# A fused retention and snake-activation kernel on one core: a new hand-written order for the first three blocks, a different order inside the loop, and a re-cut last tile

## The chip, the cores and the metric

The kernel runs on one core of one Trainium2 chip. The metric is the device time in microseconds of one execution. The program is one long instruction stream per engine: TensorE (PE, with PEld for its weight loads), VectorE (DVE), ScalarE (ACT), GpSimd (POOL) and SyncE (SP), which here issues most DMAs. Each engine runs its own stream strictly in order and waits on semaphores for the others.

## The reference

```python
def _attn_ref(q, k, v):                      # 8 batches, 8 heads, 576 tokens, 64 wide
    scores = (1 / sqrt(64)) * q @ k^T
    gamma = 1.0 - 2.0 ** (-5.0 - arange(H))  # one decay per head
    Dmat = where(rel >= 0, gamma ** rel, 0)  # rel = position of query - position of key
    return (scores * Dmat) @ v

def _moe_ref(x, w_in, w_out, alpha):         # x: 4608 tokens x 512
    h = x @ w_in                             # 512 x 2048
    s = sin(alpha * h)
    g = h + s * s / (alpha + 1e-09)
    return g @ w_out                         # 2048 x 512
```

Inputs and output are float32. The attention output of all heads, put side by side, is x.

## The kernel before, in words

**Tiling.** The 4608 tokens are nine blocks of 512. Block n (0 to 7) is the first 512 tokens of batch n; block 8 is the last 64 tokens of all eight batches (the class `Ends`). The attention is written as linear attention over chunks of 128 tokens: inside a chunk it is scores, a causal mask and values; between chunks it is a running state. The class `Attention` holds the pieces of one batch, each a burst of small TensorE matmuls of 64x64 weights: `scores(p, y)` for half p of the batch and half y of the heads (16 matmuls, L318), `outer` for the sums k^T v of the chunks (L266), `values(p, False)` and `values(p, True)` for the masked scores times v (16 matmuls each, L356), and `add_states(p)` for the contribution of the running state (L374). VectorE masks the scores (`masked`, L329). `evict`, `take_sum`, `next_sum`, `more`, `to_state` and `chain` turn the sums of the chunks into states, on ScalarE, VectorE or GpSimd. `keep` casts the result into `xT`, the input of the block's projection.

The two `values` of one half write the same PSUM bank from the two halves of the rows of the PE array; `values(p, False)` must be finished before `values(p, True)` begins. The kernel before has TensorE itself wait there: `change_rows` issues `nc.tensor.drain()`.

**The dense part.** A block has 16 units. `project(n, u)` is 4 matmuls of 512 columns (L486), `sine` is ScalarE (L494), `square` is on an engine of choice (L503 or L505), `product` is VectorE (L510) and writes `gT`. `gemm2(n, u)` is 4 matmuls (L530); four of them make one tile of 128 rows of output, which `finish` copies out of PSUM (L102 or L104) and sends by two DMAs of 64 partitions each (L523).

**Loads.** `load` brings 512 KB of q, k or v in float32 by a DMA on SP into one of six `raw` buffers (L113); `cast` scales it to float16 and frees the buffer (L161, L104). For batches 0 and 1, q and k are transposed by TensorE (`turn`, then `take` copies out); from batch 2 on by a transposing DMA on SP (`crossed`, L184). The weights come in eight pieces by DMAs on the GpSimd queue (`load_w_in` L92, `load_w_out` L95). `wait_for_w_out(g)` is a small DMA on SP that reads piece g of `w_out`, so SP goes no further before that piece has landed (L558). `keep_busy` issues matmuls on a tile of zeros whose results nobody reads (L543).

**PSUM.** Eight banks: the tag `hp` with three buffers of one bank, the tag `mm` with two buffers of two banks, the tag `op` with one bank. The buffer of a tag is the next free one.

**Order.** All of it is in a manual schedule: every engine takes its instructions in the order of the program text. Blocks 0 to 2, with the attention of batches 0 to 3 and the loads up to batch 4, are one list written out by hand (L561 to L1024). Blocks 3 to 8 are a loop (L1026 on): block n projects, the second GEMM of block n-1 follows one block behind, and the attention of batch n+1, the loads and casts of batch n+2 and the ends are hung at given units with `at_unit` (before the unit's activation work) and `behind` (after it). In the loop before, a batch's attention sits at units 0, 4, 8 and 12; its chunk sums are at unit 4:

```python
at_unit(4, lambda: A.outer((0, 1)), lambda: A.scores(1, 0), lambda: A.evict((0, 1)))
behind(4, lambda: A.chain((0, 1, 2, 3)), lambda: A.masked(1, 0))
at_unit(8, lambda: A.scores(1, 1), lambda: A.values(0, False))
at_unit(12, lambda: A.values(1, False), lambda: A.values(0, True), lambda: A.add_states(0))
```

After the loop come the 16 second-GEMM units of block 8; the last unit is cut into two column halves in one PSUM bank.

Of the kernel before, what the change touches and what calls it, by code (L numbers as in the profile page):

```python
# [1 line left out]

# [14 lines left out]
def kernel(  # L17
# [170 lines left out]
    def turn(b, nm, p, ys=(0, 1), tag="hp"):  # L188
        if (b, nm, p) not in trs:
            trs[b, nm, p] = psum.tile([P, 1024], F16, tag=tag, bufs={"hp": 3, "op": 1}[tag], name="tr")  # L190
# [18 lines left out]
    turns = nc.alloc_semaphore("turns")  # L209
    turn_of = {}  # L210
    unmarked = []

# [9 lines left out]

    class Attention:
        def __init__(self, b):
            self.b = b
            self.both = {}
            self.o = {}
            self.ret = {}
            self.sc = {}
            self.kv = {}  # L230
            self.tiles = {}

# [17 lines left out]
        def outer(self, ps, spare=False):  # L250
            b = self.b
            if spare:
                kv = [
                    psum.tile([P, 512], F32, tag=tag, bufs=3 if tag == "hp" else 1, name="kv")
                    for tag in ("op", "hp")
                ]
            else:
                kv2 = psum.tile([P, 2, 512], F32, tag="mm", bufs=2, name="kv")
                kv = [kv2[:, g] for g in range(2)]
                self.kv2 = kv2  # L260
# [14 lines left out]
        def evict(self, ps, eng=None):  # L275
# [4 lines left out]
                self.kv2[:, :, 0 : 256 * N].rearrange("p g (x y) -> p g x y", x=N),  # L280
            )
# [27 lines left out]
        def scores(self, p, y):  # L309
            kT, qT = T[self.b, "k", p], T[self.b, "q", p]  # L310
            sc = psum.tile([P, 2, 512], F32, tag="mm", bufs=2, name="sc")
# [25 lines left out]
        def values(self, p, same, spare=False):  # L337
# [3 lines left out]
            else:  # L341
                open_turns.append((self, p))
            if p not in self.o and spare:
                self.o[p] = [psum.tile([P, 512], F32, tag="hp", bufs=3, name="o") for t in range(2)]
            elif p not in self.o:
                self.both[p] = psum.tile([P, 2, 512], F32, tag="mm", bufs=2, name="o")
                self.o[p] = [self.both[p][:, t] for t in range(2)]
            o, v16 = self.o[p], half[self.b, "v", p]
            for x in range(2):
                for r in range(2):  # L350
                    for e in range(2):
                        for g in range(2):
# [3 lines left out]
                            matmul(  # L356
# [4 lines left out]
                            )  # L361
# [32 lines left out]
    class Ends:  # L394


        def __init__(self, j0):
            self.js = (j0, j0 + 1)
            self.o = {}

        def scores(self):
            self.sc = psum.tile([P, 2, 512], F32, tag="mm", bufs=2, name="scs")
# [22 lines left out]
        def values(self, w, same):  # L425
            if same:
                change_rows((self, w))
            else:
                open_turns.append((self, w))
            if w not in self.o:  # L430
                self.o[w] = psum.tile([P, 2, 512], F32, tag="mm", bufs=2, name="os")
            o, v16 = self.o[w], half[2 * self.js[w], "v", 2]
            for x in range(2):
                for e in range(2):
                    for g in range(2):
                        t = g if same else 1 - g
                        c = 128 * x + 64 * g
                        matmul(
                            o[halves(e), t, c : c + 64],
                            v16[halves(g), 4 * t + 2 * x + e, :],  # L440
                            self.ret[halves(g), t, w, 2 * x + e, :],
                            start=(not same and x == 0), stop=False, skip_group_check=True,
                        )

        def add_states(self, w):
            o, j = self.o[w], self.js[w]
            for g in range(2):
                for x in range(2):
                    for e in range(2):
                        for t in range(2):  # L450
                            c = 128 * x + 64 * g
                            matmul(
                                o[halves(e), t, c : c + 64],
                                sS[halves(t), 2 * j + g, 2 * x + e, :],
                                T[2 * j, "q", 2][halves(t), 2 * x + e, halves(g)],
                                start=False, stop=True, skip_group_check=True,
                            )

        def keep(self, w, eng):
# [4 lines left out]
                self.o[w][:, :, 0:256].rearrange("p t (x n) -> p t x n", x=2),  # L464
# [8 lines left out]
    def bank(tag):  # L473
        if tag == "mm":
            return psum.tile([P, 2, 512], F32, tag="mm", bufs=2, name="hps")[:, 0]
        return psum.tile([P, 512], F32, tag=tag, bufs=3 if tag == "hp" else 1, name="hps")

    def project(n, fc, part=None, tag="hp"):
# [33 lines left out]
    def rows_of(n, c, h):  # L512
        if n == 8:
            b = 2 * c + h
            return out[576 * b + 512 : 576 * b + 576, :]
        r0 = 576 * n + 128 * c
        return out[r0 : r0 + 128, :].rearrange("(i r) d -> r i d", r=2)[h]

    def finish(n, c, eng=None, cols=slice(0, 512)):
        osb = work.tile([P, 512], F32, tag="osb", bufs=4, name="osb")  # L520
        copy(eng or nc.scalar, osb[:, cols], ops[n, c][:, cols])
        for h in range(2):
            nc.sync.dma_start(rows_of(n, c, h)[:, cols], osb[halves(h), cols])  # L523

    def gemm2(n, u, tag="op", cols=slice(0, 512)):
        c, part = divmod(u, 4)
        if (n, c) not in ops:
            ops[n, c] = psum.tile([P, 512], F32, tag=tag, bufs=1 if tag == "op" else 3, name="ops")
        for fk in range(4 * part, 4 * part + 4):
            matmul(  # L530
                ops[n, c][:, cols], gT[n][:, fk, c * P : (c + 1) * P], w_out16[:, fk, cols],
                start=(fk == 0 and cols.start == 0), stop=(fk == FC - 1), skip_group_check=True,
# [7 lines left out]
    def keep_busy(n, m=512, tag="op"):  # L540
        idle = psum.tile([P, 512], F32, tag=tag, bufs=3 if tag == "hp" else 1, name="idle")
# [18 lines left out]
    with tc.manual_schedule():  # L560
# [9 lines left out]

        load(0, "k", 0)
        load(0, "q", 0)
        load(0, "k", 1)
        load(0, "q", 1)
        load(0, "v", 0)
        load(0, "v", 1)
        keep_busy(13)
        cast(0, "k", 0, V)
        turn(0, "k", 0)
        take(0, "k", 0, A_)  # L580
        keep_busy(2)
        cast(0, "q", 0, V)
        turn(0, "q", 0)
        take(0, "q", 0, V)
        keep_busy(2, tag="hp")
        at[0].scores(0, 1)
        turn_alpha()
        cast(0, "k", 1, V, (0,))
        cast(0, "k", 1, G_, (1,))
        load_w_in(0)  # L590
        take_alpha()
        at[0].scores(0, 0)
        turn(0, "k", 1)
        take(0, "k", 1, A_)
        at[0].masked(0, 0)
        cast(0, "q", 1, G_)
        load_w_in(2)
        load_w_in(1)
        keep_busy(6)
        cast(0, "v", 0, A_)  # L600
        at[0].masked(0, 1)
        turn(0, "q", 1)
        take(0, "q", 1, A_, (1,))
        take(0, "q", 1, V, (0,))
        at[0].outer((0,), spare=True)
        keep_busy(3, tag="hp")
        at[0].take_sum(0, A_)
        cast(0, "v", 1, A_)
        at[0].take_sum(1, V)
        at[0].more(1)  # L610
        at[0].to_state(1, G_)
        at[0].to_state(0, G_)
        load_w_out(0)
        load_w_in(3)
        at[0].scores(1, 0)
        at[0].scores(1, 1)
        at[0].masked(1, 0)
        at[0].masked(1, 1)
        load_w_out(1)
        keep_busy(5, tag="hp")  # L620
        at[0].outer((1,), spare=True)
        at[0].values(0, False)
# [3 lines left out]
        at[0].next_sum(2)  # L626
        at[0].to_state(2, V)
        at[0].values(1, False, spare=True)
        at[0].values(1, True, spare=True)
        at[0].add_states(1)  # L630
        invert_alpha()
        at[0].keep(1, V, A_)
        wait_for_w_out(0)
        load(1, "k", 0)
        load(1, "q", 0)
# [3 lines left out]
        load(2, "k", 0)  # L639
        project(0, 1, 0, tag="mm")  # L640
        project(0, 0, 0, tag="mm")
        project(0, 0, 1, tag="mm")
        sine(0, 0)
        at[0].next_sum(3)
        project(0, 1, 1, tag="mm")
        sine(0, 1)
        load_w_out(2)
        at[0].to_state(3, G_)
        project(0, 2, tag="op")
        sine(0, 2)  # L650
        square(0, 2, A_)
        square(0, 1, V)
        square(0, 0, V)
        project(0, 3)
# [466 lines left out]
```

## Time and profile before

| what | us |
|---|---|
| median of 3 runs (range) | 319.76 (319.76 to 322.72) |
| the profiled execution's own time | 320.69 |
| its span, first to last instruction | 318.9 |
| TensorE busy | 301.3 (94%) |
| VectorE, ScalarE, GpSimd busy | 216.9, 174.0, 137.3 |
| first projection matmul of block 0 | starts at 19.89 |
| projections of block 1 in full swing | from 59.17 |
| first projection of the loop (block 3) | 115.52 |
| blocks 3, 4, 5, 6 of the loop | 31.62, 31.58, 31.58, 31.56 each |
| last second-GEMM stretch begins | 299.44 |
| end | 318.9 |

The span is 1.79 us shorter than the execution's own time; the rest lies before the first and after the last instruction. Times inside the span are read against 318.9. TensorE's matmuls are pipelined: a matmul of 512 columns is shown with 0.38 us, and in an unbroken stream four of them start every 0.864 us, which is 0.216 us each.

### The profile page before, as it was taken

The numbers are of one execution on the slowest core, as the hardware profiler recorded it, in microseconds if no ns is written. First come the engines' busy times: TensorE is split into PE (matmuls) and PEld (weight loads), VectorE is DVE, ScalarE is ACT, GpSimd is POOL, SyncE is SP. The second block draws the span as 40 slices with busy tenths as digits, with TensorE's granted clock in tenths as the row PEclk, the third lists the DMA queues.
The fourth block names the chain that finished last, engine by engine and source line by source line (L and its number), as shares of the span: only waits on it lengthen the run. The fifth ranks groups of instructions, "written<-read, shape, count | busy, mean of one in ns | idle before, by whom it ended". The sixth has DMA issues, their size and how long they took to land.

```text
span 318.9 us, 7711 instructions
## 1 busy us (share of the span) xinstructions
PE 301.3 (94%) x3180; PEld 143.9 (45%) x3180; DVE 216.9 (68%) x316; ACT 174.0 (55%) x269; POOL 137.3 (43%) x140
## 2 busy tenths in 40 slices
PE   7889999699799999999999999999999999999994
PEld 2554454244344444444444444444444444444442
DVE  2778877669468989687878787878746565655500
ACT  3548654498356645464547454745465565456411
POOL 0866542472866961993299329922720000000000
PEclk9999999799999999999999999999999999999999
DMA  8999999999994559996999589952352111111232
GB/s 211 266 202 209 299 242 280 218 239 232 213 248 144 84 113 251 262 171 134 245 255 184 123 240 257 155 113 67 72 82 49 35 35 33 36 33 34 57 77 66
DMA packets 103108, 49.96 MB, mean 157 GB/s; under 512 B 44944, under 2 KB 98592, under 8 KB 103072
## 3 DMA queue, kind: packets, MB, share of 16 engines
q1 hardware_dynamic: 98352, 45.12, 63.1%
q0 software_dynamic: 4224, 4.19, 8.0%
q8 instruction: 25, 0.41, 0.6%
q10 hardware_dynamic: 496, 0.15, 0.2%
q14 instruction: 11, 0.09, 0.1%
HBM read 36.85 MB, written 9.44 MB: 145 GB/s over the span
## 4 chain that ended last, share of the span: by engine, by line
PE 78%; DMA 9%; DVE 6%; ACT 2%; POOL 2%; issue 2%; ACTq 0%; POOLq 0%; DVEq 0%
PE hps L486 35%; PE ops L530 34%; DMA v<-in_v_dram 5%; DMA q<-in_q_dram 3%; PE sc L318 2%; PE o L356 2%; DVE gT L510 2%; DVE ret L329 2%; DVE ss_t L505 1%; DMA k<-in_k_dram 1%; PE kv L266 1%; ACT s_t L494 1%; PE o L374 1%; PE idle L543 1%; ACT ss_t L503 1%
## 5 line engine op out<-in xcount | busy, mean ns | idle before, releaser
L494 ACT ACTIVATE s_t<-hps,alpha_t 128x512 f16<-128x512 f32 x144 | 97.9, 685 | 97.1 <-PE hps L486 96.7
L530 PE MATMUL ops<-w_out,gT 128*128 128x512 f16 x580 | 144.0, 378 | 0.9 <-ACT osb L102 0.5
L510 DVE SCALAR_TENSOR_TENSOR gT<-ss_t,inva,hps 128x512 f16<-128x512 f16 x144 | 106.1, 746 | 49.4 <-ACT ss_t L503 42.1
L486 PE MATMUL hps<-xT,w_in 128*128 128x512 f16 (+1 forms) x520 | 129.3, 380 | 3.6 <-DVE xT L104 2.1
L486 PEld LDWEIGHTS <-w_in 128*128 128x128 f16 x584 | 56.8, 98 | 71.2 <-issue 5.9
L530 PEld LDWEIGHTS <-gT 128*128 128x128 f16 x580 | 54.3, 98 | 64.5 <-DVE gT L510 0.9
L505 DVE TENSOR_TENSOR ss_t<-s_t 128x512 f16<-128x512 f16 x88 | 54.0, 614 | 17.3 <-ACT s_t L494 17.2
L329 DVE TENSOR_TENSOR ret<-sc,mask 128x1024 f16<-128x1024 f32 x32 | 38.6, 1218 | 1.7 <-PE sc L318 1.6
L293 POOL TENSOR_TENSOR s<-kvs,cn 128x256 f16<-128x256 f32 x20 | 13.4, 670 | 49.4 <-ACT kvs L102 47.1
L161 POOL TENSOR_TENSOR k<-k,cn 128x1024 f16<-128x1024 f32 (+1 forms) x13 | 24.8, 1911 | 17.3 <-DMA k<-in_k_dram 17.3
L102 ACT COPY osb<-ops 128x512 f32<-128x512 f32 (+1 forms) x36 | 20.5, 573 | 16.8 <-PE ops L530 14.2
L503 ACT ACTIVATE ss_t<-s_t 128x512 f16<-128x512 f16 x45 | 28.3, 631 | 0.6
L161 POOL TENSOR_TENSOR q<-q,cn 128x1024 f16<-128x1024 f32 (+1 forms) x15 | 27.3, 1822 | 1.1 <-DMA q<-in_q_dram 1.0
L102 ACT CAST xT<-o 128x1024 f16<-128x1024 f32 (+1 forms) x16 | 13.6, 881 | 13.0 <-PE o L374 12.8
L505 POOL TENSOR_TENSOR ss_t<-s_t 128x512 f16<-128x512 f16 x11 | 11.3, 1039 | 13.4 <-ACT s_t L494 12.7
L486 PE MATMUL hps<-xS,w_in 128*128 128x512 f16 x64 | 16.4, 379 | 0.0
L104 POOL CAST v<-v 128x1024 f16<-128x1024 f32 (+1 forms) x12 | 13.0, 1084 | 6.5 <-DMA v<-in_v_dram 6.5
L301 POOL TENSOR_TENSOR kvs<-s,kvs 128x256 f32<-128x256 f32 x19 | 15.1, 792 | 1.5
L356 PE MATMUL o<-ret,v 64*64 64x128 f16 x512 | 13.0, 220 | 1.8 <-issue 0.6
L300 POOL TENSOR_TENSOR s<-kvs,cn 128x256 f32<-128x256 f32 x19 | 12.1, 635 | 2.8 <-ACT kvs L102 2.7
L318 PE MATMUL sc<-qT,kT 64*64 64x128 f16 x512 | 12.1, 220 | 0.7 <-DVE qT L104 0.4
L356 PEld LDWEIGHTS <-v 64*64 64x64 f16 x512 | 8.8, 106 | 7.9 <-issue 7.8
(52 smaller groups left out, 126.7 us busy)
## 6 DMA issues: line engine op xcount, KB each, us to landing
out_dram<-osb SPq DMA_DIRECT2D x70, 128.0 KB, 2.4
k<-in_k_dram SPq DMA_DIRECT2D x16, 512.0 KB, 6.7
q<-in_q_dram SPq DMA_DIRECT2D x16, 512.0 KB, 6.4
v<-in_v_dram SPq DMA_DIRECT2D x16, 512.0 KB, 7.1
w_in<-in_moe_w_in_dram POOLq DMA_DIRECT2D x4, 512.0 KB, 8.1
w_out<-in_moe_w_out_dram POOLq DMA_DIRECT2D x4, 512.0 KB, 10.0
ks<-in_k_dram SPq DMA_DIRECT2D x8, 128.0 KB, 5.8
qs<-in_q_dram SPq DMA_DIRECT2D x8, 128.0 KB, 3.8
```

The lines of the kernel that those rows point to most:

```text
L102: eng.copy(d_, s_)
L161: eng.tensor_tensor(dst[:, a0:a1].rearrange("p a r t d -> p t (a r) d"), t_.rearrange("p (t a) x -> p t a x", t=2)[:, :, a0:a1].rearrange( ...
L301: nc.gpsimd.tensor_tensor(self.kvs[:, c], s32, self.kvs[:, c], ADD)
L318: matmul(sc[halves(g), t, c : c + 128], kT[halves(t), 2 * a + r, halves(g)], qT[halves(t), 2 * a : 2 * a + 2, halves(g)], start=(z == 0 an ...
L329: nc.vector.tensor_tensor(ret.rearrange("p t (z x) -> p (t z) x", z=2), sc.rearrange("p t (z x) -> p (t z) x", z=2), mask[:, 0:256].unsque ...
L356: matmul(o[t][halves(e), c : c + 128], v16[halves(g), 4 * t + 2 * x + e, r, :], self.ret[p, x][halves(g), t, m : m + 128], start=(not same ...
L486: matmul(hps_of[n, fc][0][:, cols], w_in16[:, a, fc * P : (fc + 1) * P], xs[n][:, a, cols], start=(a == 0 and part != 1), stop=(a == KT - ...
L494: nc.scalar.activation(s_t, hps, mybir.ActivationFunctionType.Sin, bias=0.0, scale=alpha_t[:, fc : fc + 1],)
L503: nc.scalar.activation(ss_t, s_t, mybir.ActivationFunctionType.Square)
L505: eng.tensor_tensor(ss_t, s_t, s_t, MULT)
L510: nc.vector.scalar_tensor_tensor(gT[n][:, fc, :], ss_t, inva[:, fc : fc + 1], hps, MULT, ADD)
L530: matmul(ops[n, c][:, cols], gT[n][:, fk, c * P : (c + 1) * P], w_out16[:, fk, cols], start=(fk == 0 and cols.start == 0), stop=(fk == FC ...
```

## The change

The change has five parts.

1. A new list for blocks 0 to 2, with the same operations, apart from the engine of some of them, the halves in which some are done, and the order. Every PSUM tile now names its bank or pair: `h0`, `h1`, `h2`, `op` (one bank each), `m0`, `m1` (two banks each), one buffer per tag.
2. In the loop, the chunk sums (`outer`) of batch n+2 move to unit 12 of block n, between the `values(p, False)` and the `values(p, True)` of batch n+1. From block 4 on the scores are issued at units 3 and 8. The squares of units 4, 5, 6, 8 and 9 move from VectorE to ScalarE, and the second-GEMM units 12 and 13 are issued together at unit 13. Loads and casts move to other units.
3. In the loop, the TensorE drain is replaced by a SyncE `nop` that depends on the last matmul of `values(p, False)` and on which the first matmul of `values(p, True)` depends.
4. `Ends` puts the results of its two halves into one pair of banks, and its bursts go from four places to two.
5. An output tile is sent by one DMA of 128 partitions. The last tile is computed as two column halves in two banks, each over all 16 slices, and the second half's DMA is issued by ScalarE.

The diff, cut to its core; of the new list, the parts that are spoken of below:

```diff
+    def order(later, earlier):
+        tc.add_manual_dep(later.ins, earlier.ins.name, ...)
+    def told(last):
+        mark = nc.sync.nop()
+        order(mark, last)
+        return mark
...
-        def values(self, p, same, spare=False):
+        def values(self, p, same, *tags, relay=False):
             if same:
                 change_rows((self, p))
             else:
-                open_turns.append((self, p))
+                if not relay:
+                    open_turns.append((self, p))
...
+            if not same and relay:
+                self.mark[p] = told(made[-1])
+            elif p in self.mark:
+                order(made[0], self.mark[p])
...
-        for h in range(2):
-            nc.sync.dma_start(rows_of(n, c, h)[:, cols], osb[halves(h), cols])
+        (issue or nc.sync).dma_start(rows_of(n, c)[:, :, cols], osb[:, cols])
...
         # the new list: startup
+        load(0, "q", 0)
+        cast(0, "q", 0, G_, (1,))
+        cast(0, "q", 0, V, (0,))
+        turn(0, "q", 0, "h0")
+        load(0, "k", 0)
+        cast(0, "k", 0, G_, (0,))
+        cast(0, "k", 0, V, (1,))
...
+        cast(0, "k", 1, G_)
+        load(0, "q", 1)
+        cast(0, "q", 1, V)
+        load_w_in(0)
...
+        cast(0, "v", 0, G_)
+        at[0].outer((0,), "op", "h0")
+        load_w_in(1)
...
+        load_w_in(2)
+        load(1, "q", 0)
...
+        project(0, 0, "m1", 0)
+        load(1, "k", 0)
+        at[0].keep(1, A_, V)
+        project(0, 0, "m1", 1)
...
         # block 0 to block 1
+        at[1].keep(1, A_)
+        at[1].keep(0, V, A_)
...
+        gemm2(0, 15, "op")
+        gemm2(0, 3, "h1")
+        project(1, 2, "m1")
...
         # casts and transposes of batches 2 and 3
+        cast(2, "k", 0, G_)
+        at[1].to_state(2, V)
+        cast(3, "k", 1, G_, (1,))
+        load(2, "v", 0)
+        load(2, "q", 0)
+        cast(2, "q", 0, G_)
+        cast(2, "v", 0, G_)
+        load(2, "k", 1)
+        cast(2, "k", 1, G_)
+        load(2, "q", 1)
+        cast(2, "q", 1, G_, (0,))
+        cast(2, "q", 1, G_, (1,))
+        load(3, "k", 0)
+        crossed(2, 0, "k")
+        cast(3, "k", 0, G_)
+        crossed(2, 0, "q")
+        load(2, "v", 1)
+        cast(2, "v", 1, G_)
...
         # the loop
+                    at_unit(3, lambda: A.scores(0, 0, next(m)), lambda: A.scores(0, 1, next(m)))
+                    at_unit(8, lambda: A.scores(1, 0, next(m)), lambda: A.scores(1, 1, next(m)))
...
+                at_unit(12, lambda: A.values(0, False, next(m), relay=True), lambda: A.values(1, False, next(m), relay=True))
+                if n < 6:
+                    at_unit(12, lambda: at[n + 2].outer((0, 1), "op", next(h)))
+                at_unit(12, lambda: A.values(0, True), lambda: A.add_states(0), lambda: A.values(1, True), lambda: A.add_states(1))
...
+                E = (Ends(0), Ends(2))
+                at_unit(1, lambda: E[0].scores(next(m)), lambda: E[1].scores(next(m)))
+                at_unit(8, lambda: E[0].values(False, next(m)), lambda: E[1].values(False, next(m)))
+                at_unit(8, lambda: E[0].values(True), lambda: E[1].values(True))
...
-        for u in range(15):
-            gemm2(NBLK - 1, u, "hp")
-            if u % 4 == 3:
-                finish(NBLK - 1, u // 4)
-        for cols in (slice(0, 256), slice(256, 512)):
-            gemm2(NBLK - 1, 15, "hp", cols)
-            finish(NBLK - 1, 3, cols=cols)
+        for c in range(3):
+            tag = next(h)
+            for u in range(4 * c, 4 * c + 4):
+                gemm2(NBLK - 1, u, tag)
+            finish(NBLK - 1, c)
+        for cols, issue in ((slice(0, 256), nc.sync), (slice(256, 512), nc.scalar)):
+            tag = next(h)
+            for u in range(12, 16):
+                gemm2(NBLK - 1, u, tag, cols)
+            finish(NBLK - 1, 3, cols=cols, issue=issue)
```

More of the change, by code (lines that the diff above doesn't have):

```diff
@@ L423, in masked @@
             )
[L425 to L443, printed above, removed]
@@ L608 @@
[L608 to L622, printed above, removed]
+        cast(0, "q", 1, V)
+        load_w_in(0)
+        turn(0, "k", 1, "h1")
@@ L625 @@
         at[0].keep(0, A_)
[L626 to L629, printed above, removed]
+        at[0].values(1, False, "h2", "h0")
+        at[0].values(1, True)
         at[0].add_states(1)
-        invert_alpha()
[L632 to L635, printed above, removed]
+        project(0, 0, "m1", 0)
+        load(1, "k", 0)
+        at[0].keep(1, A_, V)
+        project(0, 0, "m1", 1)
+        take_alpha()
+        sine(0, 0)
+        cast(1, "q", 0, V, (1,))
+        cast(1, "q", 0, V, (0,))
+        square(0, 0, V)
+        invert_alpha()
+        product(0, 0)
+        project(0, 6, "h1")
+        sine(0, 6)
+        square(0, 6, V)
+        project(0, 2, "m0")
+        sine(0, 2)
+        product(0, 6)
+        project(0, 3, "h2")
+        sine(0, 3)
+        square(0, 3, A_)
+        project(0, 5, "h0")
+        sine(0, 5)
+        project(0, 1, "op")
+        project(0, 7, "m1", 0)
+        sine(0, 1)
+        square(0, 1, A_)
+        square(0, 2, V)
+        product(0, 2)
+        product(0, 3)
+        cast(1, "k", 0, V, (1,))
+        product(0, 1)
         load(1, "k", 1)
@@ new lines @@
+        crossed(3, 0, "q")
+        gemm2(0, 15, "op")
+        gemm2(0, 3, "h1")
+        project(1, 2, "m1")
+        load(3, "v", 0)
+        sine(1, 2)
+        square(1, 2, A_)
+        finish(0, 0)
+        at[1].to_state(3, V)
+        finish(0, 3, V)
+        product(1, 2)
+        project(1, 5, "op")
+        project(1, 7, "h2")
+        sine(1, 7)
+        square(1, 7, V)
+        gemm2(0, 7, "h0")
+        finish(0, 1)
+        sine(1, 5)
+        square(1, 5, V)
+        product(1, 7)
@@ L889 @@
+        at[2].to_state(1, V)
+        at[2].values(0, False, "m1")
         at[2].values(0, True)
-        at[2].masked(1, 1)
-        sine(1, 15)
-        square(1, 15, A_)
+        at[2].add_states(0)
+        at[2].keep(0, A_)
         product(1, 15)
-        at[2].to_state(0, G_)
-        at[2].more(1)
-        at[2].more(2)
-        at[2].to_state(1, G_)
+        at[2].to_state(2, G_)
+        cast(3, "v", 1, G_)
         at[2].more(3)
         at[2].to_state(3, G_)
-        gemm2(1, 2)
-        gemm2(1, 4, "hp")
@@ L997 @@
-        project(2, 12)
-        sine(2, 12)
-        at[3].values(1, False)
+        at[3].masked(0, 1)
+        at[2].keep(1, V)
+        gemm2(1, 7, "h1")
+        cast(3, "v", 0, A_, (0,))
+        cast(3, "v", 0, G_, (1,))
+        project(2, 1, "op", 0)
+        finish(1, 1, V)
+        project(2, 2, "m0", 0)
+        project(2, 2, "m0", 1)
+        project(2, 3, "m1")
+        sine(2, 3)
+        gemm2(1, 8, "h2")
+        project(2, 5, "h0")
+        project(2, 1, "op", 1)
+        sine(2, 2)
@@ new lines @@
+        square(2, 2, A_)
+        gemm2(1, 9, "h2")
+        at[3].scores(0, 0, "m1")
+        sine(2, 1)
+        at[3].outer((0, 1), "m0")
+        square(2, 3, V)
+        project(2, 7, "h1")
+        product(2, 3)
+        product(2, 2)
+        sine(2, 5)
+        square(2, 5, G_)
+        square(2, 1, V)
+        product(2, 1)
+        at[3].masked(0, 0)
+        at[3].evict((0, 1), A_)
+        at[3].more(1)
+        at[3].more(2)
+        product(2, 5)
+        cast(4, "q", 0, G_, (1,))
@@ new lines @@
+        load(4, "v", 0)
+        sine(2, 7)
+        square(2, 7, A_)
+        product(2, 7)
+        cast(4, "k", 0, G_, (0,))
+        at[3].to_state(2, G_)
+        cast(4, "q", 0, G_, (0,))
+        project(2, 11, "op")
+        cast(4, "k", 0, V, (1,))
+        sine(2, 11)
+        crossed(4, 0, "q")
+        project(2, 0, "m0")
+        at[3].to_state(0, G_)
+        crossed(4, 0, "k")
+        square(2, 11, V)
+        sine(2, 0)
+        square(2, 0, A_)
+        product(2, 0)
+        gemm2(1, 10, "h2")
@@ L1015 @@
+        sine(2, 6)
+        square(2, 6, G_)
+        project(2, 8, "op")
+        gemm2(1, 15, "h2")
+        sine(2, 8)
+        square(2, 8, V)
+        product(2, 6)
+        finish(1, 3)
+        project(2, 14, "h0")
+        product(2, 8)
         sine(2, 14)
```

816 lines of the change are left out of this document (388 added, 428 removed).

## The prediction

> **What bounds the kernel now.** I read the page first, then the busy time of each engine by stage.
>
> ```profile
> span 318.9 us, 7711 instructions
> PE 301.3 (94%) x3180; PEld 143.9 (45%) x3180; DVE 216.9 (68%) x316; ACT 174.0 (55%) x269; POOL 137.3 (43%) x140
> ```
>
> ```profile
> core 0: us, PE busy (x) PEld busy (x) DVE busy (x) ACT busy (x) POOL busy (x), PEclk, DMA share, GB/s
> 0.00:19.89 19.89, 15.49 (x280) 8.16 (x281) 11.51 (x20) 7.65 (x11) 10.55 (x17) 1.00 1.05 230
> 19.89:39.50 19.61, 18.92 (x100) 9.49 (x100) 15.83 (x28) 13.84 (x22) 10.35 (x10) 1.00 1.20 243
> 39.50:59.17 19.67, 15.95 (x286) 8.65 (x286) 15.26 (x26) 8.51 (x14) 8.90 (x8) 1.00 1.13 263
> 59.17:87.40 28.23, 25.27 (x290) 11.07 (x293) 18.61 (x26) 19.68 (x31) 15.48 (x16) 0.94 1.01 219
> 87.40:115.52 28.12, 27.49 (x337) 12.77 (x337) 22.90 (x30) 17.35 (x27) 22.26 (x22) 1.00 0.72 153
> ...
> 147.14:178.72 31.58, 31.48 (x346) 15.12 (x344) 24.78 (x32) 17.96 (x28) 19.73 (x19) 1.00 0.89 202
> ```
>
> From 115.52 on TensorE is busy 31.48 of 31.58 us in a block: the loop is bound by what TensorE executes. Before that it idles 0.7, 3.7, 3.0 and 0.6 us in the four stretches after startup. The chain that ended last names the worst place:
>
> ```profile
> 48.18 8.28 DMA q<-in_q_dram
> ...
> 58.44 0.69 DVE xT L104
> ...
> 59.17 7.47 PE hps L486 x26
> ```
>
> A load of q is late, VectorE stands at its cast with the `keep` of block 1's input queued behind, and TensorE has run out of second-GEMM units. The 26 matmuls that follow take 7.47 us where 26 x 0.216 = 5.62 is the stream rate; the clock of that stretch is 0.94. The stall is paid twice.
>
> **The loop, from its bursts.** The critical chain gives 0.864 us for four 512-column matmuls, so a block's 128 cost 27.65. The rest of 31.58 is 3.92 in four bursts, from the starts in the timeline. The one at unit 12:
>
> ```profile
> 171.24 0.93 PE L356 MATMUL o<-ret,v 64*64 64x128 f16 x32
> 172.00 0.29 PE L374 MATMUL o<-qT,s 64*64 64x128 f16 x8
> 172.11 0.40 PE L356 MATMUL o<-ret,v 64*64 64x128 f16 x16
> 172.33 0.40 PE L374 MATMUL o<-qT,s 64*64 64x128 f16 x16
> ```
>
> The stream would have gone on at 171.14 and does so at 172.66: 1.52 us for 72 matmuls. The score burst at unit 0 gives the price of one: 32 in 0.57 us, 0.0178 each, with 0.10 lost on entering. So unit 12 is 0.10 + 1.28 and 0.14 for the drain. The chunk sums are 64 in 0.58. Before: 0.67 (unit 0), 1.06 (unit 4), 0.67 (unit 8), 1.52 (unit 12). After, blocks 4 and 5: 0.67, 0.67, and at unit 12 88 matmuls, 1.57 + 0.58 + 0.10 = 2.25; sum 3.59, 0.33 saved. Block 3 keeps its three places and carries the sums of two batches: 0.67 + 1.06 + 0.39 + 2.25 = 4.37, 0.45 lost. Block 6 has no sums: 0.67 + 0.67 + 1.67 + up to 0.14 of hop = about 3.1, 0.8 saved. Block 7's four bursts cost 0.47, 1.01, 0.47 and 1.01; two bursts of the same matmuls lose two entries and about 0.25 of drains: 0.45 saved. Loop: -0.45 + 0.66 + 0.8 + 0.45 = **1.5 us saved**.
>
> That takes the hop over SyncE at nothing. What hides it is the 0.58 of chunk sums (in block 6 only the 0.28 of the second `values(p, False)`). A hop is 0.07 us in the chain (0.03 of queue, 0.04 of issue, at 313.70), two make 0.14. The `nop` stands in SP's queue behind the output DMA of unit 11, issued 0.6 us after the copy; copy (0.59) and issue end 1.3 us after the second GEMM of unit 11, while project (0.86) and the two `values` (0.67) take 1.5: SP is free by 0.2. If that cover went, SP would hold the `nop` for the length of a DMA issue, 0.6 to 1.8 us in the loop, with TensorE's `values(p, True)` and all behind it waiting. The squares moved to ScalarE bring it to 16 x 0.685 + 9 x 0.63 + 4 x 0.59 + about 3.2 of copies = 22 of 31.5 us; VectorE falls. Both hide under TensorE. The chunk sums need `op` and one more bank: `op` is copied out 0.7 us after unit 11, before the sums begin at 1.5. The casts they need are hung at units 3 to 6, six units (over 10 us) ahead. I take 0 for these; the lower end is a loss of 1 us a block.
>
> **The end.** Now the copy of the first column half stands between two sets of matmuls, and SP issues four DMAs:
>
> ```profile
> 313.77 0.37 ACT L102 COPY osb<-ops 128x256 f32<-128x256 f32 x1 [2.48 <-PE ops L530]
> 314.16 2.38 SPq L523 DMA_DIRECT2D out_dram<-osb  x4
> 314.19 0.60 PE L530 MATMUL ops<-w_out,gT 128*128 128x256 f16 x4 [0.50 <-ACT osb L102]
> 314.87 0.37 ACT L102 COPY osb<-ops 128x256 f32<-128x256 f32 x1 [0.73 <-PE ops L530]
> ```
>
> Two banks take the wait away: the last matmul ends at 313.70 + 0.43 = 314.13 instead of 314.80, the 32 half-width matmuls costing the same 3.46 us as 16 wide ones. Then a copy to 314.57 and one DMA issue (0.45 to 0.6) to 315.1, where the last issue ended at 316.54: 1.4 us. A DMA of 128 KB lands 2.4 us after its issue, of 64 KB 2.0. I take **1.3 us saved**, between 0.9 and 1.5.
>
> **The list, up to block 1.** Startup: the first five loads land 1.9 us apart (4.97 to 12.6), whichever comes first. Following the new order with the durations of the rows, POOL finishes the cast of k's second half at 11.1, issues the first piece of `w_in` (before: 10.1), casts v to 13.9 and 15.9, and `more` and `to_state` put the second half's states at 20.0; the first projection starts at 20.4, against 19.89. From 21.4 on VectorE has no gap in sight: 16 products at 0.69, six squares at 0.43, four half casts at 0.70, copies and inverse 1.5, together 18, to 39.4; then four masks at 1.22, three states and a cast: 46.0. The remaining values, states and two second-GEMM units are 3.4 us on TensorE: block 1 starts at 49.4 if nothing waits. The stretch from 19.89 to 39.5 has 3.8 us of idle VectorE, that after it 4.4. I put the first in and not the second, since in the new order the loads of batch 1 start as soon as buffers come free (at about 9 us; now SP stands at the gate until 25.5): 53.2. Five second-GEMM units (4.3 us) are then still to do, which the old order had done: 57.5 against 59.17, **1.7 saved**. Ends: 5.5 saved with no wait, 2.7 lost with both.
>
> **The list, blocks 1 and 2.** 59.17 to 115.52 is 56.35 us; the work in it is 48 units x 0.864 = 41.5, two batches at 152 x 0.0178 + 0.58 = 3.29 each, and some 13 entries at 0.10: 49.4. So 7.0 us are lost, 1.85 of them to the clock after the stall. The new order has second-GEMM units of block 0 standing between the last `keep` and the projections of block 1 (1.7 us of cover for two copies that take 1.7), so this stall should go. For the other waits (on products, on states, 0.3 to 1.3 us each) the list is as dense as before, and GpSimd has more: by count times row, 71 us up to the loop instead of 62. I take half of the 7.0: **3.5 saved**, between 7.0 and -3.
>
> **Sum.** 1.5 + 1.3 + 1.7 + 3.5 = 8.0 us. The profiled span would be 318.9 - 8.0 = 310.9, its execution 320.69 - 8.0 = 312.7, and against the median 319.76 - 8.0 = **311.8 us**. The median is 0.93 below the profiled execution, which no step here depends on.
>
> [...]
>
> **Rivals.** *All waits go.* Then 5.5 + 7.0 + 1.5 + 1.3 = 15.3: 304.5. VectorE speaks against it, which would have to work without a gap. 10%.
>
> *The waits only move.* Seven microseconds of waits come back at other places of the list; loop and end remain: 319.76 - 2.8 = 317.0. For it: VectorE has 86 us of work ahead of the loop by count, the same as before (87). 18%.
>
> *SyncE goes round in circles: slower.* In the new list the casts of batches 2 and 3 are nearly all GpSimd's, and SP's transposes stand between the loads, so a load waits behind a transpose, that for a cast, that for a load. Before, the load of k of batch 3 is issued at 51.30 and the last transpose of batch 4 at 117.15: 66 us for 12 loads at 1.8, 12 transposes at 1.9 and 16 output DMAs at 0.6, 54 in all, so 12 are slack. A full trip is 7.1 us to land and 1.9 to cast instead of 3.7 of issue: 5.3 more. Two trips fit into the slack; the third costs 4; four put the loop 9 us late, and the list's gain is gone: 319.76 + 9 - 2.8 = 326. Against it: the loads stand two or three ahead of their transposes. 13%.
>
> *GpSimd holds VectorE up.* A square on VectorE that met a cast on GpSimd took 1.62 us (at 35.75, beside the cast from 35.19 to 37.09), against 0.42 alone. With 9 us more of GpSimd, eight such meetings, 1.2 each, cost 9.6: the list loses 4.4 in place of gaining 5.2, 321.4. 5%. [...]
>
> *The word over SyncE comes late*, so that the change does not do what it says: 1.8 us in each of four blocks, 311.8 + 7.2 + 0.5 for the drains = 319.5. 4%.
>
> **How the numbers follow.** The forecast has 50%, with a range of its own from 308 to 316. The range 306 to 322 leaves out the slow trips and half of the first rival, 19%. One per cent, 3.2 us, is about what a measurement can tell from no change. Faster by that: the forecast, the first rival and a quarter of the second, 65%; within it: the rest of the second, the two small rivals, 20%; slower: 15%.
>
> **What would show it.** Right: first projection near 20.4; no wait of TensorE over 1 us between the last `keep` of block 1's input and its projections, and the clock at 1.00 there; the loop begins near 110; blocks 4 and 5 at 31.25, block 6 at 30.8, and no gap between `outer` and `values(p, True)`; 4.7 us or less from the last wide matmul to the end. Wrong: VectorE idle over 4 us between 21 and 46, SP waiting for GpSimd's casts over 12 us ahead of the loop, or a block of the loop above 31.6 other than block 3.

## The result, and the profile after

The changed kernel takes **376.0 us** (median of 4 runs, 375.08 to 377.52) where the kernel before takes 320.24 (4 runs, 319.76 to 322.72): a ratio of 1.173, 95% interval 1.165 to 1.180. The forecast was 311.8, the range 306 to 322.

The page of the changed kernel, its first lines and its DMA line in 40 slices of 9.35 us:

```profile
span 373.9 us, 7789 instructions
PE 308.7 (83%) x3238; PEld 155.2 (42%) x3238; DVE 206.8 (55%) x283; ACT 184.1 (49%) x292; POOL 139.6 (37%) x151
...
DMA  8999999939878999489553976387238111111111
```

TensorE's busy time has grown by only 7.4 us, the span by 55.0: TensorE waits. The work by stage follows. Up to 119.70 it is cut at the first projections of the blocks; in the loop the cuts 161.70 and 204.60 stand behind the bursts of unit 12 of blocks 3 and 4, and the last row begins 1.2 us after the last copy:

```profile
core 0: us, PE busy (x) PEld busy (x) DVE busy (x) ACT busy (x) POOL busy (x), PEclk, DMA share, GB/s
...
55.05:85.73 30.68, 29.80 (x369) 16.04 (x368) 24.84 (x31) 20.57 (x33) 23.93 (x24) 1.00 0.82 179
...
119.70:161.70 42.00, 29.48 (x382) 14.48 (x380) 21.15 (x28) 19.52 (x31) 20.57 (x23) 0.86 0.79 145
161.70:204.60 42.90, 32.80 (x348) 15.99 (x344) 21.41 (x27) 21.09 (x34) 18.74 (x19) 0.90 0.71 148
...
358.80:373.80 15.00, 0.00 (x0) 0.00 (x0) 0.00 (x0) 0.00 (x0) 0.00 (x0) 0.60 0.12 45
```

Up to 85.73 next to nothing is held up: block 1 begins at 55.05 (forecast 53.2, with five second-GEMM units still to do). Then the stages grow. From one burst of unit 12 to the next it is 42.90 us, where a block before takes 31.6, and in the two rows of the loop TensorE does nothing for 12.5 and 10.1 us. The last row is the strangest. No engine has any work left, and the output still flows for 15 us, at 45 GB/s and a DMA share of 0.12, which is what 2 of 16 DMA engines would give (2/16 = 0.125).

In the loop the wait stands just where the change put the word over SyncE. Two of the bursts at unit 12, from the timeline of TensorE:

```profile
152.36 0.64 PE L374 MATMUL o<-ret,v 64*64 64x128 f16 x32
152.83 0.71 PE L275 MATMUL kv<-v,k 64*64 64x64 f16 x64
160.06 0.64 PE L374 MATMUL o<-ret,v 64*64 64x128 f16 x16 [6.51 <-SPq L230]
...
203.07 0.64 PE L374 MATMUL o<-ret,v 64*64 64x128 f16 x16 [10.10 <-SPq L230]
```

After the chunk sums (L275) TensorE waits 6.51 and 10.10 us for the `nop` of line 230; the third, of block 5, waits 9.00, and that of block 6, which has no chunk sums, 0.17. That is 25.8 us which the profile puts down to SyncE. It invites the verdict that the word is the fault. SyncE's own timeline ahead of 160.06 and the chain of waits ahead of 203.07 say more:

```profile
146.32 4.01 SPq L121 DMA_DIRECT2D ks<-in_k_dram  x2
...
151.18 4.35 SPq L121 DMA_DIRECT2D qs<-in_q_dram  x2
155.57 2.49 SPq L121 DMA_DIRECT2D vs<-in_v_dram  x2
158.16 1.79 SPq L544 DMA_DIRECT2D out_dram<-osb  x1
```

```profile
190.24 8.00 DMA ks<-in_k_dram
198.37 1.05 POOL ks L146
...
200.60 2.35 SPq L544
203.07 0.64 PE o L374 x12
```

SyncE issues DMAs with hardly a pause here, 1.2 to 2.2 us each, and the `nop` is at the end of that queue. In the chain ahead of it stands a load of 128 KB (`ks`) that needs 8.00 us to land. So the DMAs themselves may be what is slow, and the word only one of those who feel it.

### The profile page after: what moved, and what is told of

The parts are those of the page before. It is cut to its first block, busy times and chain, and to the rows that moved or that the text cites. A ratio compares the mean times of both kernels' runs of the same rounds, so it can differ in the third digit from the quotient of the medians.

```text
span 373.9 us, 7789 instructions
## 1 busy us (share of the span) xinstructions
PE 308.7 (83%) x3238; PEld 155.2 (42%) x3238; DVE 206.8 (55%) x283; ACT 184.1 (49%) x292; POOL 139.6 (37%) x151
## 3 DMA queue, kind: packets, MB, share of 16 engines
HBM read 36.85 MB, written 9.44 MB: 124 GB/s over the span
## 4 chain that ended last, share of the span: by engine, by line
PE 59%; DMA 16%; SPq 9%; POOL 4%; DVE 3%; issue 2%; ACT 2%; ACTq 0%; POOLq 0%; DVEq 0%
PE ops L551 28%; PE hps L509 23%; SPq L121 4%; DMA ks<-in_k_dram 4%; DMA kT<-k 4%; DMA w_out<-in_moe_w_out_dram 3%; PE o L374 3%; PE sc L334 3%; SPq L544 2%; DMA v<-in_v_dram 2%; DMA qT<-q 2%; DVE gT L533 2%; SPq L114 1%; DMA q<-in_q_dram 1%; PE o L396 1%
## 5 line engine op out<-in xcount | busy, mean ns | idle before, releaser
L551 PE MATMUL ops<-w_out,gT 128*128 128x512 f16 (+1 forms) x592 | 147.3, 381 | 1.6 <-DMA w_out<-in_moe_w_out_dram 1.5
L509 PEld LDWEIGHTS <-w_in 128*128 128x128 f16 x632 | 61.8, 99 | 67.4 <-issue 5.9
L551 PEld LDWEIGHTS <-gT 128*128 128x128 f16 x592 | 57.2, 100 | 68.1 <-issue 7.6
L528 DVE TENSOR_TENSOR ss_t<-s_t 128x512 f16<-128x512 f16 x67 | 40.0, 597 | 55.1 <-ACT s_t L517 54.8
L162 POOL TENSOR_TENSOR k<-k,cn 128x1024 f16<-128x1024 f32 (+1 forms) x17 | 29.3, 1724 | 47.7 <-DMA k<-in_k_dram 32.4
L526 ACT ACTIVATE ss_t<-s_t 128x512 f16<-128x512 f16 x69 | 43.4, 633 | 1.6 <-DVE gT L533 0.5
L374 PE MATMUL o<-ret,v 64*64 64x128 f16 x512 | 14.2, 242 | 27.1 <-SPq L230 25.8
L162 POOL TENSOR_TENSOR q<-q,cn 128x512 f16<-128x512 f32 (+1 forms) x16 | 24.4, 1530 | 16.1 <-DMA q<-in_q_dram 15.8
L317 POOL TENSOR_TENSOR kvs<-s,kvs 128x256 f32<-128x256 f32 x23 | 17.2, 747 | 18.7 <-ACT kvs L103 17.2
L334 PEld LDWEIGHTS <-kT 64*64 64x64 f16 x512 | 8.8, 113 | 20.8 <-issue 10.9
L105 POOL CAST v<-v 128x1024 f16<-128x1024 f32 (+1 forms) x15 | 15.3, 1017 | 3.0 <-DMA v<-in_v_dram 2.9
```

The costliest lines, as they stand in the source:

```text
L162: eng.tensor_tensor(dst[:, a0:a1].rearrange("p a r t d -> p t (a r) d"), t_.rearrange("p (t a) x -> p t a x", t=2)[:, :, a0:a1].rearrange( ...
L317: nc.gpsimd.tensor_tensor(self.kvs[:, c], s32, self.kvs[:, c], ADD)
L334: matmul(sc[halves(g), t, c : c + 128], kT[halves(t), 2 * a + r, halves(g)], qT[halves(t), 2 * a : 2 * a + 2, halves(g)], start=(z == 0 an ...
L374: made.append(matmul(o[t][halves(e), c : c + 128], v16[halves(g), 4 * t + 2 * x + e, r, :], self.ret[p, x][halves(g), t, m : m + 128], sta ...
L509: matmul(hps_of[n, fc][0][:, cols], w_in16[:, a, fc * P : (fc + 1) * P], xs[n][:, a, cols], start=(a == 0 and part != 1), stop=(a == KT - ...
L526: nc.scalar.activation(ss_t, s_t, mybir.ActivationFunctionType.Square)
```

## The experiments

**The word, the DMA, both, and the DMA alone on the kernel before.** The two suspects are the `nop` (part 3) and the single output DMA (part 5). Two DMAs per tile again:

```diff
-        (issue or nc.sync).dma_start(rows_of(n, c)[:, :, cols], osb[:, cols])
+        for h in range(2):
+            (issue or nc.sync).dma_start(rows_of(n, c)[h][:, cols], osb[halves(h), cols])
```

> The changed kernel, but an output tile is again sent by two DMAs of 64 partitions (a 256 KB tile has 2 x 64 rows). Theory A, the output DMA: one DMA whose outermost dimension is 2 is carried by few of the 16 DMA engines, so its 256 KB take long there and every later load and transpose, which needs all 16, lands behind it; the late word of SyncE, the late transposes and the late end all follow. A expects 311 to 322 us here, the waits of TensorE for SyncE under 1 us in all and the end within 5 us of the last copy. Theory B, the word: SyncE's nop stands behind slow DMA issues whatever the output looks like; B expects 345 to 365 us and still over 15 us of waits for SyncE.

Measured: 313.91, ratio 0.978 (0.975 to 0.981). One edit of one line gives back 62.1 us and makes the kernel faster than before.

TensorE's drain in place of the word, the single DMA kept:

```diff
-    at_unit(12, lambda: A.values(0, False, next(m), relay=True), lambda: A.values(1, False, next(m), relay=True))
+    at_unit(12, lambda: A.values(0, False, next(m)), lambda: A.values(1, False, next(m)))
```

and in `Ends.values` the calls of `order` and `told` give way to `change_rows` and `open_turns`.

> The changed kernel, but TensorE drains itself between the two values of a half, in the loop and in the ends, instead of waiting for SyncE's nop; the single output DMA is kept. A expects 340 to 360 us: the 26 us of waits for SyncE go, the late loads and transposes ahead of and in the loop and the 15 us from the last copy to the end stay. B expects 315 to 325 us.

Measured: 374.48, ratio 1.165 (1.162 to 1.169). The 340 to 360 us expected there was missed. All 25.8 us of waiting for SyncE are gone, and the time falls by 1.5. The list of waits of this kernel shows where they went (columns: us in total, times, longest):

```profile
PE sc L334 <- DMA qT<-q: 27.2, 4, 9.6
...
PE sc L334 <- DMA kT<-k: 6.6, 2, 3.7
```

The scores now wait 33.8 us for the transposes of q and k, where in the changed kernel it was 7.2 and 6.0. Most of the wait was only moved.

Both edits together:

> Both undone: two output DMAs and the drain. A expects the time of the run with two output DMAs and the word, within 2 us. B expects that of the run with the drain and one output DMA.

Measured: 315.04, ratio 0.981 (0.978 to 0.984). Beside e1_two_dmas the word is worth 1.1 us, as a gain.

The kernel before, with nothing but the single DMA:

```diff
-        for h in range(2):
-            nc.sync.dma_start(rows_of(n, c, h)[:, cols], osb[halves(h), cols])
+        nc.sync.dma_start(rows_of(n, c)[:, :, cols], osb[:, cols])
```

> The kernel before with one thing of the change: each output tile in one DMA of 2 x 64 rows. A expects 335 to 380 us, slower by over 15, with loads and transposes landing later than the 3.9 to 7.1 us of before. B expects 318 to 322 us, no change.

Measured: 376.71, ratio 1.173 (1.169 to 1.176). Its last stretch in the windows:

```profile
358.80:373.80 15.00, 0.00 (x0) 0.00 (x0) 0.00 (x0) 0.00 (x0) 0.00 (x0) 0.60 0.12 45
```

It is the row of the changed kernel, to the digit. An old list with an old loop, a new list with a new loop, and a new list with a drain all end within 2.3 us of each other (376.71, 376.0, 374.48). Neither the order of the list, nor that of the loop, nor the word changes the time by more than that, once the single DMA is there.

**The outermost dimension.** Theory A supposes that the outermost dimension of the transfer decides how many engines carry it. If so, the same 256 KB in one DMA must become cheap when that dimension grows. The output DMA of blocks 0 to 7 goes as 4 x 32 rows, then as 16 x 8, so that the rows of a tile land in another order in the output; block 8 has two DMAs of 64 rows in both:

```diff
+        if n < 8:
+            r0 = 576 * n + 128 * c
+            rows = out[r0 : r0 + 128, cols].rearrange("(i q) d -> q i d", q=4)    # or q=16
+            (issue or nc.sync).dma_start(rows, osb[:, cols])
+            return
```

> The changed kernel with its single DMA of 256 KB per tile for blocks 0 to 7, but the 128 partitions go to the rows as 4 x 32 instead of 2 x 64 (the rows of a tile then lie in another order in the output; block 8 has two DMAs of 64 rows). Bytes, row length and number of DMAs are those of the change. Theory A: the outermost dimension sets how many DMA engines carry the transfer; with 4 of them each carries half of what it does with 2, the backlog all but goes: 312 to 335 us. Rival C: a single DMA of 128 partitions is slow whatever its shape: 365 to 380 us.

> The same with 16 x 8. A: all 16 engines carry it; 311 to 315 us, as with two DMAs. C: 365 to 380 us.

Measured: 328.22, ratio 1.024 (1.019 to 1.030), with 4; 313.3, ratio 0.977 (0.972 to 0.982), with 16. With 4 TensorE still waits 9.2 us for the `nop`, in three places; with 16 there is nothing left to see of it. In the lines of DMA issues the 32 output DMAs of 256 KB as 16 x 8 rows land 3.5 us after their issue (median), the 70 of 128 KB in e1_two_dmas after 2.6.

So it is neither the size of the transfer nor the number of issues: one DMA of 256 KB is as good as two of 128 KB if its outermost dimension is 16. The factor is the outermost dimension: 2, 4 and 16 give 376.0, 328.2 and 313.3. The two DMAs of block 8 are not what helps: up to the last second-GEMM stretch, behind which block 8's tiles come, the three kernels need 342.24, 308.23 and 292.69 us.

The rates bear it out. The DMA view from 285 to 305 us (40 slices of 0.5 us), where little but output moves, with 4 and then with 16:

```profile
DMA  2222200000132122222000001221222210000012
GB/s 61 74 106 102 86 25 0 0 0 0 25 25 12 25 61 82 111 98 78 8 0 16 0 0 29 20 12 29 66 90 102 98 74 4 0 0 0 0 37 12
...
DMA  0000000685000000000008820000993000199200
GB/s 0 0 0 0 0 0 0 143 217 197 0 0 0 0 0 0 0 0 0 0 0 176 250 98 0 0 0 16 209 213 86 0 0 0 49 201 213 62 0 0
```

Full slices have a share of two tenths and about 100 GB/s with 4, and of nine tenths and 201 to 213 with 16. With 2 they have one tenth and about 50 (below).

The last half tile alone as one DMA of 2 x 64 rows, everything else as two:

```diff
+        if issue is nc.scalar:
+            issue.dma_start(rows_of(n, c)[:, :, cols], osb[:, cols])
+            return
```

> Two DMAs of 64 partitions per tile everywhere, but the very last half tile, issued by ScalarE, goes by one DMA of 2 x 64 rows, 128 KB. A: two engines at 45 GB/s, as in the last 15 us of the changed kernel, take 2.9 us where 16 take 0.2 to 0.5; one issue of 0.6 is saved: 1 to 3 us more than with two DMAs there, 315 to 317 us. If the prediction's step for the end was right in its sign: 0.5 less, 313.4 us.

Measured: 317.11, ratio 0.989 (0.985 to 0.994), at the upper edge of the 315 to 317 expected. Here a slow DMA stands alone, with no queue behind it. The end in the timeline of this kernel:

```profile
309.02 0.37 ACT L103 COPY osb<-ops 128x256 f32<-128x256 f32 x1 [1.38 <-PE ops L555]
309.42 1.12 ACTq L545 DMA_DIRECT2D out_dram<-osb  x1
```

From the end of the copy (309.39) to the end of the span (315.3) are 5.9 us, where e1_two_dmas has 308.49 to 312.1, 3.6. 128 KB at 45 GB/s are 2.9 us of transfer, which is the order of the 2.3 lost. The 0.2 to 0.5 us expected for the fast transfer is shown by no run; at the 201 to 213 GB/s of e7_sixteen_rows it would be 0.6, an estimate. The medians differ by 3.2; the other 0.9 lies ahead of the end of the copy and is not this DMA's. The issue of this one DMA takes 1.12 us, as long as the two issues of e1_two_dmas together (1.19).

The list of the kernel before, with its own PSUM tags, and behind it the new loop, ends, word and halved last tile, with two DMAs:

> The list of before for blocks 0 to 2, and behind it the loop, the ends, the word of SyncE and the halved last tile of the change, with two DMAs of 64 partitions per tile. If list, loop and end add up as the traces of the run with two DMAs show (loop begins 5 us earlier, loop and end 1.7 us shorter): 319.0 us, between 318.3 and 319.7. If the loop's gain needs the new list: 320.5 us or more. If the list gains nothing of its own: 314 to 316 us.

Measured: 319.36 (10 runs, 315.73 to 320.74), ratio 0.994 (0.991 to 0.998). Its loop begins at 115.06 and its last second-GEMM stretch at 297.92, so loop and end take 182.86 + 18.98 = 201.84 where before they took 183.75 + 19.63 = 203.38 (split at 299.27, the same matmul; the table's 299.44 is 0.17 after it): 1.5 us. Of the 6.8 us of e1_two_dmas the other 5.3 are the new list's.

**The word only where it is covered.** In e1_two_dmas the word costs nothing in blocks 3 to 5 and something in block 6 and in the ends (below). So: word in blocks 3 to 5, drain elsewhere (in `Ends.values` as in e2_drain), and the last half tile's two DMAs on two queues. Beside it e1_two_dmas once more, on the same chip:

```diff
-    at_unit(12, lambda: A.values(0, False, next(m), relay=True), lambda: A.values(1, False, next(m), relay=True))
+    at_unit(12, lambda: A.values(0, False, next(m), relay=n < 6), lambda: A.values(1, False, next(m), relay=n < 6))
...
+        for h in range(2):
+            (issue if issue and h else nc.sync).dma_start(rows_of(n, c)[h][:, cols], osb[halves(h), cols])
```

> Two DMAs per tile; SyncE's word only in blocks 3 to 5, where the chunk sums cover it; TensorE's drain in block 6 and in the ends, where the trace of the run with two DMAs shows 0.48 and 0.62 us of waiting for the word and the run with drains everywhere shows no gap; the two DMAs of the very last half tile issued by SyncE and ScalarE, one each, instead of both by ScalarE. If these waits are on the path: 1.1 us less than with the word everywhere, and 0.3 to 0.6 for the last issue: 312.2 to 312.8 us. If the cover of TensorE's stream is such that they are made up elsewhere: 313.5 to 314.

> The changed kernel with two DMAs of 64 partitions per tile, again, beside the run before it on the same chip: 313.9 us.

Measured: 313.17, ratio 0.977 (0.974 to 0.981), and 314.58, ratio 0.982 (0.979 to 0.985): 1.4 us between them. All six runs of the one (312.76 to 313.47) lie below all six of the other (314.28 to 314.88). The first is 0.4 above the 312.2 to 312.8 expected of it. This version beats both kernels.

## Why the prediction was wrong

**The step that failed is the price of part 5.** It stands in "The end" as "one DMA issue (0.45 to 0.6)" and "A DMA of 128 KB lands 2.4 us after its issue". Three things were wrong with it. The 2.4 us was taken from DMAs of 64 partitions, whose outermost dimension in DRAM is 64; the new DMA's is 2, and its rate over the last 15 us, in which nothing else moves, is 45 GB/s. The issue it counted took 1.13 us on ScalarE (at 357.60) and not 0.45 to 0.6. And it was priced at the last tile alone. The other 35 tiles got no term at all: the text costs them neither at nothing with a cover nor at something. All 36 together cost 376.0 - 313.9 = 62 us.

How 62 us come out of it: the output is 9.44 MB, which at 45 GB/s takes 210 us. The first output DMA of the changed kernel is issued at 74.24, and the span ends at 373.9, 300 us later. In the loop a tile of 262 KB comes every four units, 7.8 us, and would need 5.8 us at 45 GB/s alone, beside all loads and transposes. From about 290 us on (the last nine slices of the page's DMA line) nothing but output moves, and it goes on for 16.3 us past the last copy. The DMA view cut to 95 to 130 us (40 slices of 0.875 us) shows what that does where loads are due:

```profile
DMA  1118999990899999911159721196112961293111
GB/s 51 51 51 187 239 290 287 290 244 19 196 308 288 293 288 292 289 47 49 49 165 260 252 68 65 51 188 53 47 43 63 286 150 22 64 169 52 23 40 51
```

Fourteen of the 40 slices run at one tenth, most of them at 40 to 65 GB/s, next to slices at 290, while loads and transposes are waiting to land. In the same window e1_two_dmas moves 6.65 MB, the changed kernel 5.18. What the other 90 of the 300 us are can be estimated up to the last load, in the windows:

```profile
74.24:286.00 211.76, 171.68 (x1880) 84.00 (x1878) 114.68 (x148) 108.45 (x168) 93.09 (x102) 0.90 0.74 134
```

At 134 GB/s this is 28.4 MB. Of it 23 output tiles are 6.0 MB, or 118 us at 51 GB/s, and the other 22.4 MB at 290 GB/s are 77. If the two only ever took turns, that would be 195 of the 212 us.

Loads and transposes on SyncE's queue land late. In the chain of the changed kernel one `kT` lands 10.12 us after its issue and one `qT` 6.95, where e1_two_dmas has medians of 4.4 and 3.5.

```profile
98.31 6.95 DMA qT<-q
...
127.47 10.12 DMA kT<-k
```

TensorE then has no scores to work on, or no word, and its clock falls too (0.86 to 0.90 in the stages above). That the outermost dimension is the cause is shown by 376.0, 328.22 and 313.3 us with 2, 4 and 16. How it acts was not shown. The profile has the mean share of 16 engines and no single engine: 0.12 with 2, two tenths in full slices with 4, nine tenths with 16. As many engines as that dimension counts, 2/16, 4/16 and 16/16, would fit these shares, which is the author's estimate from them. Nor was it shown that loads are held up because they share engines with the output, or that the two take turns.

The prediction did not look at the shape of the new DMA, 2 x 64 rows.

**The rival that had the place.** "The word over SyncE comes late" named unit 12, four blocks and SyncE's DMA issues, and priced 1.8 us each. The changed kernel shows 6.51, 10.10, 9.00 and 0.17 there. But without the word the kernel is as slow (374.48), so the rival was not the cause: the same backlog shows at another place. Its price, though, rested on issue times of 0.6 to 1.8 us from a trace in which the DMA queue did not back up, and that is what failed.

**The other steps, read in e1_two_dmas**, which is the change without its DMA shape. 8.0 us were forecast; its span is 312.1 against 318.9, 6.8 less, and its time of 313.91 lies in the forecast's own range of 308 to 316. The parts came out differently, so that the sum is in part luck. Some of its stages in the windows, with the columns as above; the last four are blocks 3, 4, 6 and 7, cut at their first projections:

```profile
21.97:54.83 32.86, 30.86 (x385) 17.56 (x381) 29.77 (x41) 20.25 (x34) 19.55 (x22) 0.97 1.17 251
...
85.50:110.44 24.94, 24.29 (x310) 12.93 (x309) 19.75 (x25) 16.41 (x25) 15.38 (x16) 1.00 0.82 167
110.44:142.36 31.92, 31.92 (x409) 15.61 (x408) 22.91 (x32) 22.83 (x36) 24.85 (x30) 1.00 0.94 198
142.36:173.48 31.12, 31.12 (x345) 15.14 (x344) 20.49 (x27) 20.95 (x34) 19.16 (x20) 1.00 0.96 211
...
204.60:235.72 31.12, 30.64 (x282) 14.55 (x281) 19.66 (x27) 20.07 (x32) 5.70 (x7) 1.00 0.40 81
235.72:266.40 30.68, 29.99 (x322) 14.16 (x320) 18.98 (x30) 16.81 (x29) 0.00 (x0) 1.00 0.16 36
```

- *The list: right in sum, wrong in its parts.* The loop begins at 110.44 (forecast near 110), 5.1 us earlier (forecast 5.2). Startup is longer than forecast, 21.97 instead of 20.4: the states were ready by 19.6, a little sooner than worked out, but TensorE took them up at 20.34, and 1.6 us of values and added states still lay between that and the projection, which the step left out. From there to block 1 it is 32.86 us, worked out as 53.2 - 20.4 = 32.8. With the five second-GEMM units still to do (4.3 us), nothing is saved up to there, where 1.7 was forecast; and blocks 1 and 2 take 55.61 - 4.3 = 51.3 against 56.35, 5.0 saved where 3.5 was taken. The clock is 1.00 there and the stall is gone, as said.
- *The loop: two thirds of the gain forecast.* 110.44 to 293.16 is 182.72 against 183.75, 1.0 saved (forecast 1.5). Block 3 takes 31.92, 0.30 more than before (forecast 0.45 more), and blocks 4 and 5 31.12 each (forecast 31.25). Block 6 takes 31.12 (forecast 30.8), and block 7 30.68 against 30.65 before, where 0.45 was to be saved. What blocks 6 and 7 lose is their wait for the word.
- *The hop over SyncE: right for one issue per tile.* The bursts of blocks 3, 6 and the ends in the timeline of TensorE:

```profile
134.75 0.71 PE L275 MATMUL kv<-v,k 64*64 64x64 f16 x64
135.40 0.42 PE L374 MATMUL o<-ret,v 64*64 64x128 f16 x16
...
228.75 0.42 PE L374 MATMUL o<-ret,v 64*64 64x128 f16 x16 [0.48 <-SPq L230]
...
252.30 0.45 PE L457 MATMUL os<-rets,vs 64*64 64x64 f16 x32 [0.62 <-SPq L230]
```

  Behind 64 chunk sums there is no wait, as forecast. In block 6, with a cover of 0.28, the hop was given up to 0.14, and the wait is 0.48; in the ends it is 0.62. The chain ahead of 228.75 shows what stands there:

```profile
228.04 0.60 SPq L545
228.64 0.05 issue
228.69 0.02 SPq L230
```

  It is the issue of the tile's second output DMA, which the change does not have. With the 16 x 8 rows, one issue per tile, the burst of block 6 has no wait:

```profile
228.21 0.96 PE L374 MATMUL o<-ret,v 64*64 64x128 f16 x48
...
229.18 0.42 PE L374 MATMUL o<-ret,v 64*64 64x128 f16 x16
```

  There block 6 takes 30.63 (205.18 to 235.81, forecast 30.8) and block 7 30.11 (to 265.92), 0.54 less than before. So these steps of the forecast hold for the queue that they assumed. A drain behind the chunk sums costs more than the word (in e3_both):

```profile
136.66 0.42 PE L374 MATMUL o<-ret,v 64*64 64x128 f16 x16 [0.35 <-issue]
```

- *The end: half of it.* From the last second-GEMM stretch on it is 18.94 against 19.63: 0.7 saved where 1.3 was forecast. With two DMAs the end has two issues on ScalarE again (1.19 us), and the forecast counted one. Both effects, the uncovered word and the second issue at the end, are what e10_word_where_covered takes out: 0.48 + 0.62 + about 0.6 = 1.7, of which 1.4 were measured.

The other rivals fell, read in e1_two_dmas. SyncE does wait 13.6 us for GpSimd's casts ahead of the loop, over the 12 given as a sign of the circle, but the loop begins at 110.44 all the same. VectorE's squares take 573 ns on average, against 614 before, so GpSimd does not hold them up more. Not all waits are gone, and they did not only move, since the list saves 5.1. By its own numbers the forecast's chance outside the range is 13 + 5 = 18%, where it says 19; nothing hangs on that.

## What to carry to other kernels

Before two DMAs are merged into one, read the shape of the merged transfer on both sides, outermost dimension first: the count of bytes and of issues was the same or better here, and 2 in that place cost 62 us of 314. A wait that names a semaphore's owner names who came last, not who is slow: look at what stands ahead of the `nop` in its queue, and take the named suspect away before believing it, as the wait may only move. An edit that touches 36 places is priced at 36 places, and an end where only DMA is left is the place to read a DMA's true rate.

## What the runs showed of the hardware that was not expected

- One DMA of 128 partitions x 2 KB whose DRAM side is 2 x 64 x 512 runs at a DMA share of 0.12 and 45 GB/s (last 15 us of the changed kernel and of e4_before_one_dma); as 4 x 32 x 512 its full slices have about 100 GB/s (e6_four_rows), and as 16 x 8 x 512 201 to 213, and it lands 3.5 us after its issue (median, e7_sixteen_rows).
- The damage is not the slow DMA's alone: 128 KB alone at the end cost 2.3 us behind the last copy (e8_last_dma_single), 36 tiles in a queue with loads and transposes 62 (376.0 against 313.9).
- In e1_two_dmas a word over SyncE between two groups of matmuls cost nothing behind 0.58 us of other matmuls (blocks 3 to 5). With 0.28 of them (block 6) it cost nothing where one output issue stood ahead of it in SyncE's queue (e7_sixteen_rows), and 0.48 where there were two, the second of 0.60 (e1_two_dmas). The drain behind the chunk sums cost 0.35 (e3_both, block 3).
